# Bias sums of a fused attention and expert kernel: first block half by half, weights spread in parts, every second sum in the scores' PSUM, and the first pair started among the sums

## The chip, the cores and the metric

One Trainium2 chip, one core in use. The metric is device microseconds of one execution; of several runs the median is given. The profile is of a further execution of the same program, with its own time.

## The reference

Attention with a learned position bias, then a dense two-layer block, then eight experts weighted by a normalised gate. What matters here is the bias and the scores:

```
rel = pos[:, None] - pos[None, :]                                  # 576 x 576
x = log1p(|rel|) / log1p(max(pos, 1))[:, None]
bias = relu(x @ w1 + b1) @ w2                                      # 32 hidden units, 8 heads
scores = q @ k^T / 8 + bias;  attn = softmax(scores)               # 2 batches, 8 heads, 576 x 64
x = attn @ v  -> dense (1152 x 512, softplus, 2048 wide) -> 8 experts (1152 x 512, relu, 1024 wide)
```

## The kernel before, in words

**Bias.** A hidden unit is active or not depending on whether a query's log position lies above a threshold that depends on the distance and the unit. For every distance the kernel makes a 0/1 *mask* (128 rows: 4 distances x 32 hidden units; columns: query positions) and multiplies it on TensorE by weights that hold `w1*w2` and `b1*w2`, split into three bf16 parts. The distances are cut into five blocks (`BLOCKS`: 0, 128, 256, 384 with 128 distances and 512 with 64), each block but the last into two halves `hf` of 16 masks, and the queries into five tiles `t` of 128 rows (t = 0 is rows 0-127, t = 2 is rows 256-383, t = 4 has 64 rows). A *unit* (block, half, tile) is 16 x 3 = 48 matmuls of 64 columns into one PSUM tile of two banks (`sums`, L248); there are 40 units. After a unit ScalarE scales one half of the PSUM tile (`evac`, L259, tile `h`, L274) and VectorE adds the other half (`store`, L278, L279). When both halves of a block are in, VectorE mirrors the tile for negative distances where needed (tile `gr`, L300) and SyncE writes to a DRAM tensor `wt[t]` (L289). When all blocks of a tile are written, `read` (L1313) brings it back, skewed, as the bias of that query tile.

Every engine works through its own queue in the order in which the program is written. `seq` (L307) is the list of units. Ahead of unit n the loop at L322 emits the masks that the pace asks for (`MASK_PACE`: 32 + 3.5 n), by ScalarE ("a", L242), by VectorE in fp32 ("d", L245) or by VectorE in fp16 ("f", L240), as the letters of `MASKS` say. The "f" masks need thresholds that GpSimd computes (`thresholds`, L149). The weights of a block are split by GpSimd (`split_weights`, L199) and spread over the four distances of a mask by four VectorE instructions (`spread_weights`, L219), both at the units that `SPLIT` names. The PSUM tiles of the sums are four (tag `pac`), which is all eight banks.

**Attention.** Eight pairs (batch, two heads) go through nine steps each, one step for one query tile and head. `qk` (L426) is the score product (tile `sps`), `soft` (L448) adds the bias and takes the exponential, `norm` (L460) divides, three steps later `transp` (L484) transposes on TensorE, and `pv` (L510) multiplies by v. `prep` (L374) splits q, k and v of a pair into a rounded and a rest part: a VectorE cast (tiles `qh`, `ks`, `vx`) and GpSimd subtractions (`ql`, `ks`, `vx`). `load` (L362) brings q and k into one buffer, tag `raw`, so k of a pair is loaded when GpSimd has read q. The pair's tiles come in the order of `TILES`, beginning with tile 1. The attention's PSUM pool is opened after the pool of the sums is closed, so nothing of it starts before the last `store`.

Later parts (dense block, experts; L876, L760) are not touched.

## Time and profile before

| | |
|---|---|
| median of three runs | 1206.01 us (1205.31 to 1209.68) |
| profiled execution | 1205.54 us, its span 1203.7 us |
| TensorE matmul busy | 1172.0 us (97% of the span) |
| VectorE, ScalarE, GpSimd busy | 761.8, 560.3, 623.2 us |
| first bias matmul, last bias matmul | 11.67 us, 88.06 us from the span's start |
| first score product | 89.66 us |

In a row of a timeline the first number is the start, the second the time until the last of the merged instructions ends, both in us; xN is how many are merged; brackets give the idle time of the engine before it and what ended it. In a row of the windows the busy time of each engine in that stretch is followed by the number of instructions, then come the granted TensorE clock (1.00 is full), the share of the DMA engines that is busy and the rate.

### The profile page before, as it was taken

What the parts mean: (1) busy time and instruction counts of PE and PEld (TensorE: products, weight loads), DVE (VectorE), ACT (ScalarE), POOL (GpSimd) and SP (SyncE); (2) the same over time, 40 slices, a digit from 0 to 9 for tenths busy, and PEclk for the clock granted to TensorE, in tenths of its full rate; (3) what the DMA queues carried; (4) which work ended last, traced back from release to release, by engine and by line L of the source; (5) the groups of instructions that cost most, each with busy time, mean ns of one, the idle gap of its engine ahead of it and who ended that gap; (6) DMA issues with size and microseconds to landing.
All of it is one profiled execution on the core that took longest, in us unless ns stands there. A gap on an engine that the chain in (4) does not pass through costs nothing.

```text
span 1203.7 us, 19061 instructions
## 1 busy us (share of the span) xinstructions
PE 1172.0 (97%) x7418; PEld 993.0 (82%) x7418; DVE 761.8 (63%) x1356; ACT 560.3 (47%) x974; POOL 623.2 (52%) x533
## 2 busy tenths in 40 slices
PE   5879999999999999999999999999999999999998
PEld 5878988988888877888888888888888888888887
DVE  9967888668888765664555455555545545554554
ACT  7867877865554546325422332342233234323321
POOL 8226777657788864543453354345335534543540
PEclk9998999999999999999999999999999999999999
DMA  4676656022232211111111111111111111111102
GB/s 121 200 215 180 191 175 210 25 70 92 84 105 75 83 54 52 39 51 35 52 54 36 35 53 53 36 45 56 40 36 53 53 36 38 54 49 36 35 1 79
DMA packets 57774, 89.93 MB, mean 75 GB/s; under 512 B 7252, under 2 KB 36436, under 8 KB 57684
## 3 DMA queue, kind: packets, MB, share of 16 engines
q1 hardware_dynamic: 57252, 88.27, 23.4%
...
## 4 chain that ended last, share of the span: by engine, by line
PE 90%; DVE 4%; ACT 1%; issue 1%; POOL 1%; DMA 1%; SPq 0%; DVEq 0%; POOLq 0%; ACTq 0%
PE sum L876 36%; PE t L760 17%; PE pv L760 8%; PE tail L850 5%; PE op L529 4%; PE pv L892 4%; PE tail L760 4%; PE sps L441 3%; PE pac L255 2%; PE tp L492 2%; PE t L778 1%; DMA raw<-in_kT_dram 1%; DVE m L245 1%; PE tail L859 1%; DVE extra L279 1%
## 5 line engine op out<-in xcount | busy, mean ns | idle before, releaser
L695 POOL TENSOR_TENSOR wu<-f,wu 128x1024 fp32r<-128x1024 f32 x77 | 187.5, 2435 | 405.1 <-ACT wu L694 404.4
L876 PE MATMUL sum<-wd,h 128*128 128x512 f32 x1536 | 364.7, 393 | 0.0
L876 PEld LDWEIGHTS sum<-wd,h 128*128 128x128 f32 x1536 | 283.4, 188 | 56.3
L911 DVE SCALAR_TENSOR_TENSOR acc<-sum,prob,acc 128x512 f32<-128x512 f32 x224 | 168.1, 751 | 147.0 <-PE sum L876 147.0
L760 PE MATMUL t<-room,wu 128*128 128x512 f32 x592 | 164.6, 390 | 0.4 <-DVE u L783 0.4
L788 ACT ACTIVATE v<-t 128x512 f32<-128x512 f32 x37 | 22.1, 597 | 246.4 <-PE t L760 246.4
L760 PEld LDWEIGHTS t<-room,wu 128*128 128x128 f32 x592 | 111.1, 188 | 24.2 <-DVE u L783 0.9
L760 PE MATMUL pv<-x,wu 128*128 128x512 f32 x444 | 113.3, 391 | 0.0
L695 POOL TENSOR_TENSOR wd<-f,wd 128x1024 fp32r<-128x1024 f32 x40 | 96.4, 2410 | 8.8 <-ACT wd L694 8.1
L760 PEld LDWEIGHTS pv<-x,wu 128*128 128x128 f32 x444 | 83.0, 188 | 17.7 <-ACT u L788 0.4
L694 ACT ACTIVATE wu<-f 128x1024 fp32r<-128x1024 f32 x77 | 81.1, 1053 | 29.5 <-POOL f L691 23.6
L876 PE MATMUL sum<-h,wd 128*128 128x512 f32 x384 | 90.9, 393 | 0.0
L255 PE MATMUL pac<-bw,m 128*128 128x64 bf16 (+1 forms) x1920 | 65.8, 198 | 22.3 <-DVE bw L228 11.7
L760 PE MATMUL t<-x,wu 128*128 128x512 f32 x296 | 85.2, 389 | 0.0
L255 PEld LDWEIGHTS <-m 128*128 128x128 bf16 (+1 forms) x1920 | 62.8, 105 | 25.1 <-issue 15.0
L876 PEld LDWEIGHTS sum<-h,wd 128*128 128x128 f32 x384 | 70.6, 188 | 14.8 <-DVE acc L909 0.5
L804 ACT ACTIVATE hl<-tail 128x256 fp32r<-128x256 f32 x40 | 15.3, 383 | 142.2 <-PE tail L859 142.2
L783 DVE TENSOR_TENSOR u<-t,u 128x512 f32<-128x512 f32 x37 | 25.6, 691 | 71.8 <-PE t L760 71.8
L909 DVE TENSOR_TENSOR acc<-sum,acc 128x512 f32<-128x512 f32 x80 | 55.1, 688 | 23.9 <-PE sum L876 23.4
L760 PEld LDWEIGHTS t<-x,wu 128*128 128x128 f32 x296 | 55.6, 188 | 11.5
L783 DVE TENSOR_TENSOR tail<-tail,v 128x512 f32<-128x512 f32 x31 | 21.7, 699 | 67.4 <-PE tail L760 67.4
L458 ACT ACTIVATE p<-p,sm 128x576 f32<-128x576 f32 x72 | 55.7, 773 | 16.2 <-DVE sm L454 10.9
...
## 6 DMA issues: line engine op xcount, KB each, us to landing
f<-in_e_w_dram SPq DMA_DIRECT2D x128, 256.0 KB, 2.9
bias<-wt SPq DMA_DIRECT2D x16, 576.0 KB, 6.2
raw<-in_w_in_dram SPq DMA_DIRECT2D x16, 512.0 KB, 3.6
raw<-in_w_out_dram SPq DMA_DIRECT2D x16, 512.0 KB, 3.5
raw<-in_qT_dram SPq DMA_DIRECT2D x16, 288.0 KB, 4.8
raw<-in_kT_dram SPq DMA_DIRECT2D x16, 288.0 KB, 4.3
wt<-extra SPq DMA_DIRECT2D x9, 512.0 KB, 5.5
...
```

The costliest lines, as they stand in the source:

```text
L255: nc.tensor.matmul(pt[0:n, g], lhs, win(w, (k * (ng + 1) + gw) * NC, [[(ng - gw) * NC, 2], [1, NC]]), start=(k == 0), stop=(k == 2))
L458: nc.scalar.activation(p, p, AF.Exp, bias=sm[:, o:o + 1], scale=-1.0, accum_out=sm[:, 2 + o:3 + o])
L529: nc.tensor.matmul(op[:, 0:n], l, r, start=(part == 0 and k == 0), stop=(part == 8))
L694: nc.scalar.activation(w[:, 0], src, AF.Copy)
L695: nc.gpsimd.tensor_tensor(out=w[:, 1], in0=src, in1=w[:, 0].bitcast(F32), op=ALU.subtract)
L760: nc.tensor.matmul(zz, wu(u)[:, a, o:o + 128], xs[xn][b][j], start=(n in (1, 2, 5) and k == 0), stop=(k == 5), skip_group_check=True)
L783: nc.vector.tensor_tensor(out=out, in0=hold[bank_], in1=hold[name], op=ALU.add)
L850: nc.tensor.matmul(zr[:, 0:256], xl[:, b, k], wu(u)[:, a, 256 * k:256 * k + 256], start=(n == 0), stop=(n == 3 * KT - 1))
L876: nc.tensor.matmul(s, lhs, rhs, start=(n == 0), stop=(n == 5))
L892: nc.tensor.matmul(r, t[:, b, 128 * f:128 * f + 128], w[:, a, f], start=(n == 0), stop=(n == 5))
L909: nc.vector.tensor_tensor(out=d, in0=o, in1=d, op=ALU.add)
L911: nc.vector.scalar_tensor_tensor(out=d, in0=o, scalar=pool["prob"][:, t, e:e + 1], in1=d, op0=ALU.mult, op1=ALU.add)
```

## The change

Nothing of the arithmetic changes. The units are reordered: block 0 goes through all tiles with its first half, then with its second (`SEQ0`); block 3 (the last) ends with tile 0 instead of tile 3. Masks are emitted later (16 + 4 n, never more than the buffers that are free), in 14 buffers instead of 15. A block's weights are spread by one VectorE instruction at each of four units instead of four at one. Units with even n up to 36 take their PSUM from the two tiles of the scores (tag `s` of a pool that is opened first), the others from two tiles of their own. Attention becomes a generator: its first score product is emitted at unit 37, its step 0 at unit 38, its step 1 at unit 39. The first pair starts with tile 2. The table of the exponential is loaded after unit 33. `load` of the second pair's q is asked for earlier. Memsets of `vx` cover half the columns.

```diff
-TORDER = ((2, 4, 0, 3, 1), (0, 2, 4, 1, 3), (0, 1, 4, 2, 3), (1, 0, 4, 3, 2), (1, 3, 0, 4, 2))
-HF_MAJOR = (0, 1, 0, 0, 0)
-MASK_BUFS = 15
+TORDER = ((2, 4, 0, 3, 1), (0, 2, 4, 1, 3), (0, 1, 4, 2, 3), (3, 4, 1, 0, 2), (1, 3, 0, 4, 2))
+SEQ0 = ((0, 2), (0, 4), (0, 0), (0, 3), (0, 1), (1, 2), (1, 4), (1, 0), (1, 3), (1, 1))
+MASK_BUFS = 14
-MASK_PACE = (32, 3.5)
+MASK_PACE = (16, 4)
-SPLIT = (5, 13, 21, 26)
-PREP0 = (28, 31, 33, 34, 36)
-READS = ((4, 2), (1, 3), (3, 4), (0, 3), (2, 3))
+SPLIT = (4, 13, 21, 25)
+PREP0 = ((31, 0), (32, 2), (33, 1), (34, 3), (36, 4))
+OWN = tuple(range(1, 36, 2)) + (37, 38, 39)
+EARLY_G = 28
+AHEAD_STEPS = 2
+FIRST_STEPS = (37, 38, 39)
+TABLE_AT = 33
+READS = ((2, 3), (3, 3), (4, 3), (1, 2), (0, 2))
+TILES0 = ((2, 0), (2, 1), (3, 0), (4, 0), (3, 1), (1, 0), (0, 0), (0, 1), (1, 1))
+PVFIRST = (0, 0, 4, 7)
+PREPS1 = (1, 2, 6, 6, 7, 7)
+NORM0 = "aaapapppa"
...
-        bufs = [pool.tile([128, 3 * (128 // JJ + 1) * H * JJ], BF16, name=f"bw{n}") for n in range(4)]
+        bufs = [pool.tile([128, 3 * (128 // JJ + 1) * H * JJ], BF16, name=f"bw{n}") for n in range(3)]
...
-            for jj in range(JJ):
+            for jj in parts:
...
-        def sums(b, hf, t):
+        def sums(b, hf, t, shared):
             n = rows[t]
-            pt = pp.tile([128, HG, 2 * NC], F32, tag="pac", bufs=4, name="pac")
+            pt = ps2("pac").rearrange("p o (g c) -> p (o g) c", c=2 * NC) if shared else pp.tile(
+                [128, HG, 2 * NC], F32, tag="pac", bufs=2, name="pac")
...
-                if n == at:
-                    spread_weights(BLOCK_ORDER[k])
-                    if k < 4:
+                if at <= n < at + JJ:
+                    spread_weights(BLOCK_ORDER[k], (n - at,))
+                    if n == at + JJ - 1 and k < 4:
                         split_weights(BLOCK_ORDER[k + 1])
             need = HG * (units.index((b, hf)) + 1)
-            while made < len(todo) and made < max(need, MASK_PACE[0] + MASK_PACE[1] * n):
+            free = min([units.index(x[0:2]) for x in seq[max(n - 1, 0):]]) * HG
+            room = max(need, min(MASK_PACE[0] + MASK_PACE[1] * n, free + MG * MASK_BUFS))
+            while made < len(todo) and made < room:
...
-                    if i:
-                        load(i, "kr")
+                    load(*((i, "kr") if i else (1, "qr")))
...
-        seq = [(i, t, o) for i in range(len(pairs)) for t, o in tiles]
+        seq = [(i, t, o) for i in range(len(pairs)) for t, o in (tiles if i else TILES0)]
         lows, tails = [], []
         qk(*seq[0])
         for s in range(len(seq) + LAG + 2):
+            if s <= AHEAD_STEPS:
+                yield
...
-            for k, at_r in enumerate(PREPS):
+            for k, at_r in enumerate(PREPS if i else PREPS1):
...
+        steps = attention(env, pre, biases, read, ep, bp)
+        pa = ctx.enter_context(tc.tile_pool(name="psums", bufs=1, space=PSUM))
+        late = {n: [lambda k=k: prep(0, k)] for n, k in PREP0}
+        one = cst.tile([128, 1], F32, name="one")
+        late.setdefault(TABLE_AT, []).append(lambda: nc.scalar.activation(one, ident[:, 0:1], AF.Exp))
+        for n in FIRST_STEPS:
+            late.setdefault(n, []).append(lambda: next(steps))
```

Three places of the engines' queues follow, before and after. The first is VectorE around the four instructions that spread the weights of block 1 (`bw`; `m` masks, `h` and `pac` the sum of a unit, `g` and `extra` the bias tiles it is stored to). Before:

```order
L279 TENSOR_TENSOR g_139<-pac,h 128x2x16x16 [waits Activation_49]
L240 TENSOR_SCALAR m<-bias 128x576 [waits DVE_49,Pool_49]
L279 TENSOR_TENSOR g_139<-pac,h 128x2x16x16 [waits Activation_49]
L300 COPY gr<-g_139 128x1024 [waits DVE_49]
L240 TENSOR_SCALAR m<-bias 128x576 x2
L279 TENSOR_TENSOR g_140<-pac,h 64x32x16 [waits Activation_49]
L240 TENSOR_SCALAR m<-bias 128x576 x2
L279 TENSOR_TENSOR g_140<-pac,h 64x32x16 [waits Activation_49]
L300 COPY gr<-g_140 64x1024 [waits DVE_49]
L228 TENSOR_SCALAR bw_102<-bwp 32x396 [waits Pool_49]
```

With the change:

```order
L252 TENSOR_SCALAR m<-v,col_116 128x576 x6
L289 TENSOR_TENSOR g_141<-pac,h 128x2x16x16 [waits Activation_49]
L252 TENSOR_SCALAR m<-v,col_116 128x576 x2
L289 TENSOR_TENSOR g_142<-pac,h 64x32x16 [waits Activation_49]
L252 TENSOR_SCALAR m<-v,col_116 128x576 x2
L289 TENSOR_TENSOR extra<-pac,h 128x2x16x16 [waits Activation_49]
L235 TENSOR_SCALAR bw_106<-bwp 32x396 [waits Pool_49]
L252 TENSOR_SCALAR m<-v,col_116 128x576 x2
L289 TENSOR_TENSOR extra<-pac,h 128x2x16x16 [waits Activation_49]
L235 TENSOR_SCALAR bw_106<-bwp 32x396
```

The first spreading of block 1, which waits for GpSimd's split, moves from behind 14 fp32 masks, five fp16 masks and four stores to behind ten fp32 masks and three stores.

The second place is VectorE at the end of the sums (`sps` scores, `p` and `sm` the exponential's argument and row minimum, `qh` the cast of the next pair's q). Before:

```order
L279 TENSOR_TENSOR extra<-pac,h 64x32x16 [waits DMAHW7_49,Activation_49]
L279 TENSOR_TENSOR extra<-pac,h 64x32x16 [waits Activation_49]
L279 TENSOR_TENSOR extra<-pac,h 128x2x16x16 [waits DMAHW0_49,Activation_49]
L279 TENSOR_TENSOR extra<-pac,h 128x2x16x16 [waits Activation_49]
L454 ISA p,sm<-sps,bias 128x576 [waits DMAHW5_49,DVE_49,PE_49]
L454 ISA sm 128x1
L349 CAST qh<-raw 128x1152 [waits DMAHW4_49,DMAHW3_49,DMAHW2_49]
L454 ISA p,sm<-sps,bias 128x576 [waits DMAHW7_49,PE_49]
L454 ISA sm 128x1
```

With the change:

```order
L289 TENSOR_TENSOR extra<-pac,h 64x32x16 [waits Activation_49]
L289 TENSOR_TENSOR extra<-pac,h 128x2x16x16 [waits DMAHW1_49,Activation_49]
L289 TENSOR_TENSOR extra<-pac,h 128x2x16x16 [waits Activation_49]
L462 ISA p,sm<-sps,bias 128x576 [waits DMAHW5_49,PE_49]
L462 ISA sm 128x1
L289 TENSOR_TENSOR extra<-pac,h 128x2x16x16 [waits DMAHW4_49,Activation_49]
L462 ISA p,sm<-sps,bias 128x576 [waits PE_49]
L462 ISA sm 128x1
L471 TENSOR_SCALAR sm<-sm 128x1 [waits Activation_49]
L472 RECIPROCAL sm<-sm 128x1 [waits DVE_49]
L361 CAST qh<-raw 128x1152 [waits DMAHW6_49,DMAHW2_49,DMAHW1_49]
L289 TENSOR_TENSOR extra<-pac,h 128x2x16x16 [waits Activation_49]
```

Two bias additions of the first pair (`p,sm<-sps,bias`) and the cast of the second pair's q now stand ahead of the last store.

The third place is SyncE's queue at the same point (`wt_72` to `wt_76` are the DRAM tensors of tiles 0 to 4, `raw` is the buffer of q and k). Before:

```order
L289 DMA wt_76<-extra 512x1x128 [waits DMAHW6_49,DVE_49]
L1323 DMA bias<-wt_72 128x1152 [waits DMAHW7_49,DMAHW4_49]
L289 DMA wt_75<-extra 256x1x128 [waits DMAHW0_49,DVE_49]
L289 DMA wt_75<-extra 256x1x256
L1325 DMA bias<-wt_76 64x576 [waits DMAHW6_49,DMAHW2_49]
L1326 DMA bias<-wt_76 64x512 [waits DMAHW3_49]
L1327 DMA bias<-wt_76 64x64
L1323 DMA bias<-wt_75 128x1152 [waits DMAHW5_49,DMAHW1_49,DMAHW0_49]
L371 DMA raw<-in_kT_dram 64x1152 [waits DVE_49,Pool_49]
```

With the change:

```order
L299 DMA wt_76<-extra 512x1x128 [waits DMAHW5_49,DVE_49]
L1342 DMA bias<-wt_75 128x1152 [waits DMAHW6_49,DMAHW4_49,DMAHW3_49]
L299 DMA wt_73<-extra 256x1x128 [waits DMAHW7_49,DVE_49]
L1344 DMA bias<-wt_76 64x576 [waits DMAHW5_49,DMAHW0_49]
L1345 DMA bias<-wt_76 64x512 [waits DMAHW1_49]
L1346 DMA bias<-wt_76 64x64 [waits DMAHW2_49]
L299 DMA wt_72<-extra 512x1x256 [waits DVE_49]
L1342 DMA bias<-wt_73 128x1152 [waits DMAHW7_49]
L1342 DMA bias<-wt_72 128x1152 [waits DMAHW3_49]
L383 DMA raw<-in_kT_dram 64x1152 [waits DMAHW6_49,Pool_49]
```

The last tile written and the last one read are now tile 0's (a write of 512 rows of 256 numbers), with the read of tile 1 behind that write in the queue, and the second pair's k behind both reads.

## Rows read from the trace of the kernel before

**Rows 1.** Windows of 10 us: all engines, early, middle, and around the last sums

```profile
10.00:20.00 10.00, 7.53 (x108) 6.00 (x108) 9.93 (x19) 10.00 (x16) 8.62 (x18) 1.00 0.15 39
50.00:60.00 10.00, 8.85 (x297) 8.70 (x294) 9.84 (x28) 8.18 (x17) 0.00 (x0) 1.00 0.98 288
80.00:90.00 10.00, 5.62 (x163) 5.39 (x163) 2.96 (x5) 2.74 (x4) 1.38 (x4) 1.00 0.96 272
90.00:100.00 10.00, 8.28 (x44) 7.37 (x43) 6.83 (x20) 7.07 (x15) 7.42 (x12) 0.66 0.80 212
110.00:120.00 10.00, 10.00 (x71) 9.19 (x70) 7.79 (x23) 7.44 (x19) 5.57 (x8) 1.00 0.66 182
```

**Rows 2.** Timeline of PE, the last sums and the first scores

```profile
81.30 4.16 PE L255 MATMUL pac<-bw,m 128*64 128x64 bf16 x128 [1.43 <-issue]
86.94 1.12 PE L255 MATMUL pac<-bw,m 128*128 128x64 bf16 x33 [1.49 <-issue]
89.66 0.51 PE L441 MATMUL sps<-ks,qh 128*128 128x288 f32 x2 [1.59 <-DVE extra L279]
...
107.52 0.62 PE L441 MATMUL sps<-ks,qh 128*128 128x288 f32 x2
```

**Rows 3.** Timeline of POOL: split of block 1, subtraction of q

```profile
20.38 0.62 POOL L208 TENSOR_TENSOR bwf<-ac,lg 128x256 f32<-128x256 f32 x1
...
24.39 0.73 POOL L214 TENSOR_SCALAR bwp<-bwf 128x264 bf16<-128x264 f32 x1
...
69.39 2.83 POOL L389 TENSOR_TENSOR ql<-raw,qh 128x576 fp32r<-128x576 f32 x2 [21.25 <-DVE qh L349]
```

**Rows 4.** Timeline of DVE, first part of the sums

```profile
11.94 8.23 DVE L245 TENSOR_SCALAR m<-v,col 128x576 bf16<-128x576 f32 x14
...
21.80 0.69 DVE L300 COPY gr<-g 128x1024 f32<-128x1024 f32 x1
...
26.35 3.04 DVE L228 TENSOR_SCALAR bw<-bwp 32x396 int32<-32x396 int32 x4
...
50.77 0.65 DVE L240 TENSOR_SCALAR m<-bias 128x576 bf16<-128x576 f16 x2
```

**Rows 5.** Groups of DVE by form, 7.5 to 75.6 us

```profile
L240 DVE TENSOR_SCALAR m<-bias 128x576 bf16<-128x576 f16 x31 | 12.5, 441 | 0.1
```

**Rows 6.** Timeline of DVE, end of the sums and first pair

```profile
69.22 3.13 DVE L240 TENSOR_SCALAR m<-bias 128x448 bf16<-128x448 f16 x3
...
75.06 0.57 DVE L240 TENSOR_SCALAR m<-bias 128x448 bf16<-128x448 f16 x2
...
88.82 0.69 DVE L279 TENSOR_TENSOR extra<-pac,h 128x512 f32<-128x512 f32 x1 [2.36 <-ACT h L274]
...
97.60 0.76 DVE L454 CUSTOM_DVE_ANT_0 p<-sps,bias 128x576 f32<-128x576 f32 x1
...
100.98 0.76 DVE L349 CAST ks<-raw 128x1152 fp32r<-128x1152 f32 x1 [1.60 <-DMA raw<-in_kT_dram]
```

**Rows 7.** Timeline of ACT: unit 0, unit 33, unit 39

```profile
17.80 0.66 ACT L274 ACTIVATE h<-pac,rc 128x512 f32<-128x512 f32 x1
...
76.00 0.69 ACT L274 ACTIVATE h<-pac,rc 128x512 f32<-128x512 f32 x1 [0.71 <-PE pac L255]
...
88.11 0.69 ACT L274 ACTIVATE h<-pac,rc 128x512 f32<-128x512 f32 x1 [2.36 <-PE pac L255]
```

**Rows 8.** DMA issues, 60 to 112 us: size, median us to landing

```profile
bias<-wt SPq DMA_DIRECT2D x6, 576.0 KB, 5.7
wt<-extra SPq DMA_DIRECT2D x4, 512.0 KB, 6.0
...
raw<-in_kT_dram SPq DMA_DIRECT2D x2, 288.0 KB, 5.0
```

**Rows 9.** Timeline of SP: read of tile 3's bias

```profile
93.77 0.32 SPq L1323 DMA_DIRECT2D bias<-wt  x1
```

**Rows 10.** Window of 1 us: the granted clock in the first pair

```profile
92.00:93.00 1.00, 0.42 (x2) 0.07 (x1) 0.53 (x2) 0.99 (x2) 0.81 (x1) 0.50 0.98 192
```

More of the change, by code (lines that the diff above doesn't have):

```diff
@@ L133, in bias_setup @@
         nc.vector.tensor_scalar(ac[:, 1], w2c, b1c, 8.0, ALU.mult, ALU.mult)
+        cols = [pool.tile([128, S // JJ], F32, name=f"col{k}") for k in range(3)]
+        nc.vector.tensor_scalar(cols[0], lg, w1c, None, ALU.mult)
+        nc.vector.tensor_scalar(cols[1], cols[0], STEP_SCALE, None, ALU.mult)
+        nc.vector.tensor_scalar(v, v, b1c, None, ALU.mult)
+        nc.vector.tensor_scalar(cols[2], cols[0], -1.0, None, ALU.mult)
         sg = pool.tile([128, 4], F32, name="sg")
@@ L140, in bias_setup @@
         nc.vector.tensor_scalar(sign, sign, -1.0, None, ALU.add)
-        cols = [pool.tile([128, S // JJ], F32, name=f"col{k}") for k in range(3)]
-        nc.vector.tensor_scalar(cols[0], lg, w1c, None, ALU.mult)
-        nc.vector.tensor_scalar(cols[1], cols[0], STEP_SCALE, None, ALU.mult)
-        nc.vector.tensor_scalar(v, v, b1c, None, ALU.mult)
-        nc.vector.tensor_scalar(cols[2], cols[0], -1.0, None, ALU.mult)
         return v, lg, rc, cols, ac, bufs, sg
@@ L257, in sums, with evac @@
             return pt
-        def evac(b, hf, t, pt):
+        def evac(b, hf, t, pt, at):
             n, ng, size = rows[t], BLOCKS[b][1] // JJ, BLOCKS[b][1] * H
             if hf == 0:
+                while at >= EARLY_G and any(spare[0] is x for x in extra[0:2]):
+                    spare.pop(0)
                 gs[t] = spare[0]
@@ L335, in bias_emit @@
             held = ready
-            if n in late:
-                late[n]()
+            for fn in late.get(n, ()):
+                fn()
             if n == len(seq) - 1:
@@ L402, in prep @@
                     st.pop("kx")
-                    if i + 1 < len(pairs):
+                    if i and i + 1 < len(pairs):
                         load(i + 1, "qr")
@@ L416, in attention_pre, with attention @@
         return pairs, state, load, prep, fixed
-    def attention(sp, pre, biases, read, xr, beside, ep):
+    def attention(env, pre, biases, read, ep, bp):
         pairs, state, load, prep, fixed = pre
-        for w in range(2):
-            ts = [sp.tile([128, 4, 128], F32R, tag=f"v{x}{w}", name="vx") for x in "hl"]
-            for x in ts:
-                nc.gpsimd.memset(x.bitcast(F32), 0.0)
-            fixed.append(ts)
+        sp = xr = beside = None
+        made = []
         def qk(i, t, o):
@@ L462, in norm @@
             p, sm = st["p", t][:, S * o:S * o + S], st["sm", t]
-            (nc.vector if (EPS[r] if i < len(pairs) - 1 or r < 6 else EPSLAST[r - 6]) == "d" else nc.gpsimd).tensor_scalar(sm[:, 4 + o:5 + o], sm[:, 2 + o:3 + o], 1e-9, 0.0, ALU.add, ALU.add)
+            (nc.vector if (EPS[r] if i < len(pairs) - 1 or r < 6 else EPSLAST[r - 6]) == "d" or not i else nc.gpsimd).tensor_scalar(sm[:, 4 + o:5 + o], sm[:, 2 + o:3 + o], 1e-9, 0.0, ALU.add, ALU.add)
             nc.vector.reciprocal(sm[:, 6 + o:7 + o], sm[:, 4 + o:5 + o])
-            if NORM[r] == "a":
+            if (NORM if i else NORM0)[r] == "a":
                 nc.scalar.activation(p, p, AF.Copy, scale=sm[:, 6 + o:7 + o])
@@ L543, in attention @@
         for i in range(len(pairs)):
-            parts += [(i, ch, n) for ch in range(2) for n in range(9)]
+            parts += [(i, ch, n) for ch in (range(2) if i else (1, 0)) for n in range(9)]
         at, total = [], 0
@@ L555, in attention @@
         for s in range(len(seq) + LAG + 2):
+            if s <= AHEAD_STEPS:
+                yield
+            if s == AHEAD_STEPS:
+                sp, xr, beside = env
+                for w in range(2):
+                    ts = [sp.tile([128, 4, 128], F32R, tag=f"v{x}{w}", name="vx") for x in "hl"]
+                    for x in ts:
+                        nc.gpsimd.memset(x[:, :, 64:128].bitcast(F32), 0.0)
+                    fixed.append(ts)
             i, r = divmod(s, NT)
@@ L586, in attention @@
                 read(i // 2 + 1, AHEAD[i % 2, r])
-            beside(s, ep)
+            if s >= AHEAD_STEPS:
+                beside(s, ep)
     def experts(m0, accp, xr):
@@ L1331, in attention_moe_moe_kernel @@
         load, prep = pre[2:4]
-        late = {n: lambda k=k: prep(0, k) for k, n in enumerate(PREP0)}
+        env = []
+        steps = attention(env, pre, biases, read, ep, bp)
[5 more added lines that the diff above has]
+            late.setdefault(n, []).append(lambda: next(steps))
         with tc.tile_pool(name="bg", bufs=1) as gp, tc.tile_pool(name="btmp", bufs=1) as sp, tc.tile_pool(
@@ L1348, in attention_moe_moe_kernel @@
         with tc.tile_pool(name="att", bufs=1) as sp:
-            attention(sp, pre, biases, read, xr, beside, ep)
+            env += [sp, xr, beside]
+            for _ in steps:
+                pass
         top.close()
```

18 lines of the change are left out of this document (10 added, 8 removed).

## Prediction

> **What bounds the kernel now.** I read the windows first. From 110 us on TensorE is busy all 10.00 of 10 us, and it stays so through the span's 97%; between 10 and 20 us it is busy 7.53, between 80 and 90 us 5.62, between 90 and 100 us 8.28 at a granted clock of 0.66 [rows 1]. So whatever happens before about 107 us moves the rest as a block, and I need one mark there: the first score product of the second pair, which starts at 107.52 us, after which TensorE does not pause [rows 2]. Call it R. The prediction is what becomes of R.
>
> R has two parts. The last bias matmul ends at 86.94 + 1.12 = 88.06 us (call it T), and R comes 19.46 us behind it [rows 2].
>
> What sets T? In the windows VectorE is busy 9.93 of 10 us early and 9.84 in the middle, ScalarE 10.00 and 8.18, TensorE less [rows 1]. The masks' engines are the bound, not the matmuls, until the masks are done: the last mask (75.06 + 0.57 = 75.6 us) [rows 6] releases unit 33, whose evacuation starts at 76.00 [rows 7]. Then six units remain: 12.1 us to T, of which 1.43 and 1.49 us are pauses in which TensorE waited for nothing that shows [rows 2]. So T is the last mask + 12.5 us.
>
> What sets the 19.46 us? After the last unit come ScalarE's half (88.11, 0.69) [rows 7], VectorE's store (88.82 to 89.51) [rows 6], and only then the first score (89.66) [rows 2]; then the pair fills step by step, part of it at half clock (0.50 at 92 us) [rows 10], and the second pair's k is awaited until 100.98 [rows 6].
>
> **The change part by part.**
>
> *Backlog of VectorE at the start.* With half the masks needed for the first unit, ScalarE can evacuate it near 15 us instead of 17.80 [rows 7], and VectorE goes on with ten fp32 masks at 8.23 / 14 = 0.59 us [rows 4] and three stores at 0.6 us (0.69 us each, overlapping slightly) [rows 6]: 11.94 + 5.9 + 1.8 = 19.6 us. The next instruction in its queue is now the first spreading of block 1, and that waits for GpSimd's split, which before ran from 20.38 to 24.39 + 0.73 = 25.1 us [rows 3], behind the thresholds; nothing in the change moves that chain. VectorE's masks of the same and the next unit stand behind the wait, so it is idle for some 5 us. By 25.1 us the kernel before had done four more fp32 masks (4 x 0.59 = 2.3), five fp16 masks (5 x 0.32 = 1.6, price of the pair at 50.77) and one mirror copy (0.69) [rows 4]. So the change is 4.6 us of VectorE work behind. Bounds: 3 us if GpSimd, undisturbed, is done sooner and the first stores come later; 5.5 us if VectorE is there at 19.6 and everything is as before.
>
> *What comes back.* The 31 wide fp16 masks took 12.5 us together [rows 5]; at 0.32 us [rows 4] they would take 9.9, so 2.6 us were lost, while GpSimd ran its splits beside them. In the change most of them come after these splits. I give back 2.0 (bounds 0 and 2.6). Around 69 us three narrow masks took 3.13 us [rows 6] beside GpSimd's subtraction (69.39 to 72.22) [rows 3]; free they cost 0.57 / 2 = 0.28 each [rows 6], so 2.3 us were lost. In the change two masks, not three, follow the cast that releases the subtraction: I give back 0.9 (bounds 0 and 2.3). Together 2.9.
>
> The Trainium skill, "SBUF — State Buffer", section "Who interferes with whom", says that a VectorE instruction in its two-port modes and a GpSimd instruction exclude each other for the whole instruction, whichever starts first. By that rule the loss goes away wherever GpSimd is quiet, and the give-back would be nearly the whole 4.9 us, 2.0 us earlier than my sum; if the slow masks had another cause, nothing comes back and the sum is 2.9 us later. The trace agrees as far as it goes (3.13 us for three masks beside a subtraction, 0.57 us for two without).
>
> *Spreading in parts, order of units, three weight buffers, 14 mask buffers.* The counts are the same: as many masks of each kind, 20 spreadings, 40 units. I cost them at nothing. What hides them is the same VectorE queue, and the cover is thin: with a shorter lead of the masks, VectorE and ScalarE hand each other one unit at a time, and what one of them waits for the other adds up. Before, VectorE was idle 0.16 of 10 us in the middle [rows 1]. Bounds 0 and +4 us; I take 0, the value nearest to that row, and keep the rest for the range.
>
> So the last mask comes 4.6 - 2.9 = 1.7 us later. Then the six units follow as before, but two score products stand among them on TensorE, each two pairs of matmuls; a pair takes 0.51 us [rows 2], and as neighbours overlap by about half I take 0.53 for a product (1.0 at most): + 1.06. They wait for the casts of q and k and four half subtractions of 1.42 us [rows 3], 5.7 us in a row behind the last mask; TensorE comes to them 4 units of 1.5 us after it: just in time, so nothing more. T becomes 88.06 + 1.7 + 1.06 = 90.8 us.
>
> *The first pair.* Step 0 and most of step 1 are done at T, and the exponential's table is loaded before. What is late next is data, not TensorE. The last store ends 1.45 us after T (88.06 to 89.51) [rows 6] as before. Behind it SyncE writes tile 0 (512 KB, 6.0 us median [rows 8]; before, the last write was smaller and its read began 4.3 us after the store's end, at 93.77 [rows 9]): I take 5.5, so T + 7.0. Then the read of tile 0 is issued, and behind it k of the second pair: 5.0 us median [rows 8] with 0.5 us of issue, T + 12.5. Cast 0.76 [rows 6], GpSimd's first half 1.42 [rows 3], the semaphores' 0.1 each: T + 14.9. The bias of tile 0 lands between 3.8 us (93.77 to 97.60, which did not wait [rows 6, 9]) and 5.7 us [rows 8] after T + 7.0, so by T + 12.7, and its step is then 0.76 us of VectorE [rows 6], ahead of the cast: I take T + 15.3 for R, instead of T + 19.46. Bounds: T + 14 if the write takes 4.3; T + 18 if both the write and k take a microsecond more and the clock falls.
>
> The clock: TensorE was 0.42 busy at 92 us and at 0.50 of full speed, that is 1.2 instead of 2.4 GHz, after the windows in which it had been busy 5.62 of 10 us [rows 1, 10]. In the change it has gaps again between T and R. "TensorE: Matmul & The Clock Gate" in the Trainium skill, "Part 1: The HAM clock gate", says that the slow clock is the default and activity releases it. By that rule the sparse first pair may run at half clock once more; it would mostly fill idle time, and add 1 to 2 us to R. My upper bound holds it.
>
> At R one product with v (0.4 us) has not been done that was done before. R becomes 90.8 + 15.3 + 0.4 = 106.5 us instead of 107.5. That is 1.0 us less: 1204.5 us against the profiled execution's 1205.54, and 1205.0 against the median of 1206.0, which lies 0.5 above it.
>
> **The rivals.**
>
> *A, faster: the sums end when TensorE allows.* If VectorE's 5 us wait is taken up (later units have few masks, and all 4.9 us of blocking come back, and the unexplained pauses of 2.9 us fall away because other instructions stand there), T is about 88.06 + 1.06 + 4.6 - 4.9 - 2.9 = 85.9, and with T + 14, R is 100.3: 7.2 us less, 1198.8. For it: VectorE has 7 of 10 us free at 80 to 90 us [rows 1]. Against it: that time lies behind the last mask.
>
> *B, slower: the two mask engines go in step.* ScalarE's masks come in bursts (six at unit 11, five at unit 20, seven at unit 30), VectorE's in others; with four PSUM tiles and three `h` tiles between them a burst of one is waited for by the other. If the lead cannot absorb it, every unit takes the slower of the two. Counted unit by unit from unit 5 to 32 at 0.67, 0.35 or 0.56 us for a ScalarE mask and the VectorE prices above, the greater ones add up to 59.6 us, VectorE's alone to 49. Nothing absorbed: + 10.6; half of it: + 5.3, R = 111.8, 4.3 us more: 1210.3; three quarters: 1213. It decides from a last mask later than about 78.3 us (75.6 + 1.7 + the 1.0 gained). For it: both engines are near full [rows 1]. Against it: the kernel before has the same buffers and loses little.
>
> *C, the change doesn't do what it says:* the score products wait on TensorE's queue for the subtractions, and units 38 and 39 behind them. If GpSimd's chain comes 3 us late, T comes 3 us late, and the first pair no sooner: R = 109.5, 1208.
>
> **How the numbers follow.** The forecast, no change that counts: 0.62; A 0.20; B 0.13; C 0.05. The forecast's own range is the sum of its bounds taken together, not all at one end: - 4 to + 5 us, 1201 to 1210. To hold 8 in 10 it is widened to A's time and B's half: 1198.5 to 1211. About 0.5%, 6 us, is what a measurement of this kernel can tell from no change. Faster by more: A and a little of the forecast's low end, 0.22. Slower by more: B's upper part and some of C, 0.12. Within: 0.66.
>
> **What the profile after would show.** A wait of VectorE for GpSimd of 3 to 5.5 us before its first spreading of block 1, near 20 to 25 us. The wide fp16 masks' mean falling from 441 towards 330 ns. The last mask at 76 to 79 us, T at 89 to 92.5 us. The exponential's table load ahead of T. The second pair's k landing 12 to 14 us behind T, and R at 14 to 18 us behind T. I am wrong if the wait for GpSimd is absent or under 2 us, if T is earlier than 88 us, or if R comes less than 14 us behind T; and in the other direction if VectorE waits for ScalarE's `h` by more than 3 us in sum between 25 and 75 us.

## The result, and the profile after

The changed kernel takes 1216.08 us (median of five runs, 1215.32 to 1220.52) against 1205.63 for the kernel before in the same session: a ratio of 1.009, 95% interval 1.0067 to 1.0114. That is slower by 10.9 us by the ratio (10.5 by the medians), outside the range given. The profiled execution is the slowest of the five (1220.52 us, span 1218.6); by an estimate 3.4 us of its time come from a stall at 450 us (last section). The other four are 3.6 to 5.2 us faster; that they lack the stall is not shown, since they have no profile.

The windows of the changed kernel, which answer to [rows 1]:

```profile
20.00:30.00 10.00, 6.57 (x173) 6.20 (x170) 5.58 (x10) 8.17 (x14) 8.95 (x18) 0.88 0.01 2
30.00:40.00 10.00, 7.27 (x205) 6.65 (x202) 9.74 (x21) 8.47 (x15) 3.44 (x9) 0.95 0.69 197
40.00:50.00 10.00, 8.22 (x171) 7.82 (x172) 7.31 (x18) 5.87 (x9) 0.00 (x0) 0.66 0.97 302
110.00:120.00 10.00, 8.99 (x59) 7.67 (x59) 6.97 (x22) 5.72 (x13) 6.86 (x9) 1.00 0.54 162
```

Two things are new. Between 20 and 50 us VectorE and ScalarE, which were the bound, have idle time, and from 40 to 50 us TensorE's granted clock is 0.66 on average (0.50 from 42 to 48 us). And the last row, in which TensorE was busy 10.00 of 10, shows a pause: the second pair no longer runs dense.

TensorE's timeline, which answers to [rows 2] (start, length, what; in brackets the idle time before it and what ended it):

```profile
26.43 0.35 PE L263 MATMUL pac<-bw,m 128*128 128x64 bf16 x6 [3.19 <-DVE m L252]
...
38.23 0.91 PE L263 MATMUL pac<-bw,m 128*128 128x64 bf16 x15 [1.26 <-DVE m L247]
40.40 0.82 PE L263 MATMUL pac<-bw,m 128*128 128x64 bf16 x9 [1.26 <-DVE m L247]
42.56 7.61 PE L263 MATMUL pac<-bw,m 128*128 128x64 bf16 x162 [1.34 <-DVE m L247]
...
91.16 0.51 PE L448 MATMUL sps<-ks,qh 128*128 128x288 f32 x2
...
91.77 1.57 PE L263 MATMUL pac<-bw,m 128*128 128x64 bf16 x48
...
99.10 0.70 PE L448 MATMUL sps<-ks,qh 128*128 128x288 f32 x2 [2.84 <-DVE sm L462]
...
112.75 0.67 PE L448 MATMUL sps<-ks,qh 128*128 128x288 f32 x2
...
119.64 0.52 PE L448 MATMUL sps<-ks,qh 128*128 128x288 f32 x2 [0.51 <-DVE sm L471]
...
139.93 0.53 PE L448 MATMUL sps<-ks,qh 128*128 128x288 f32 x2 [0.97 <-DVE sm L471]
141.56 0.66 PE L500 MATMUL tp<-ident,p 128*128 128x128 f32 x4 [0.39 <-ACT p L474]
```

TensorE waits for masks four times early, 1.3 to 3.2 us each. T is 91.77 + 1.57 = 93.34 us (88.06 before), R is 112.75 (107.52). The pause at 139.93 comes back, with the same 0.97, at 178.96 and 217.46 us. One late instruction shows the sum, a group of transposes in the eighth pair, before and after:

```profile
226.35 0.66 PE L492 MATMUL tp<-ident,p 128*128 128x128 f32 x4 [0.35 <-ACT p L466]
```

```profile
237.77 0.66 PE L500 MATMUL tp<-ident,p 128*128 128x128 f32 x4 [0.39 <-ACT p L474]
```

11.4 us, of which 5.2 were there at R and 6.2 came behind it. Of the 6.2 the three pauses (0.97 + 0.39 or 0.40 us each) make 4.1. Another 1.8 are lost by the product of tile 4 in the second pair (124.63 us, 117.58 before), a stretch in which VectorE waits 1.69 us for the third pair's q (118.15 us below); before, that cast came at 110.18 us without a wait.

VectorE's timeline, which answers to [rows 4] and [rows 6]:

```profile
25.09 0.93 DVE L235 TENSOR_SCALAR bw<-bwp 32x396 int32<-32x396 int32 x1 [4.01 <-POOL bwp L223]
...
81.20 1.72 DVE L247 TENSOR_SCALAR m<-bias 128x448 bf16<-128x448 f16 x2
...
98.28 0.76 DVE L462 CUSTOM_DVE_ANT_0 p<-sps,bias 128x576 f32<-128x576 f32 x1 [2.89 <-DMA bias<-wt]
...
108.98 0.76 DVE L361 CAST ks<-raw 128x1152 fp32r<-128x1152 f32 x1
...
118.15 0.76 DVE L361 CAST qh<-raw 128x1152 fp32r<-128x1152 f32 x1 [1.69 <-DMA raw<-in_qT_dram]
...
139.11 0.76 DVE L462 CUSTOM_DVE_ANT_0 p<-sps,bias 128x576 f32<-128x576 f32 x1 [1.73 <-PE tps L506]
```

The wait for GpSimd's split is there with 4.01 us; the last mask ends at 82.9 us instead of 75.6. The last row is the cause of the pause on TensorE: a bias addition waits for transposes (L506) that read the score buffer it wants to write.

### The profile page after: what moved, and what is told of

Its sections match the earlier page's. It is cut to its first block, busy times and chain, and to the rows that moved or that the text cites. A ratio compares the mean times of both kernels' runs of the same rounds, so it can differ in the third digit from the quotient of the medians.

```text
span 1218.6 us, 19062 instructions
## 1 busy us (share of the span) xinstructions
PE 1176.5 (97%) x7418; PEld 995.6 (82%) x7418; DVE 762.2 (63%) x1358; ACT 562.0 (46%) x978; POOL 618.0 (51%) x527
## 4 chain that ended last, share of the span: by engine, by line
PE 89%; DVE 4%; POOL 2%; ACT 2%; DMA 1%; issue 1%; SPq 0%; POOLq 0%; DVEq 0%; ACTq 0%
PE sum L895 36%; PE t L779 16%; PE pv L779 8%; PE tail L869 4%; PE pv L911 4%; PE op L537 4%; PE tail L779 4%; PE pac L263 3%; PE sps L448 2%; PE tp L500 2%; PE t L797 1%; PE tail L878 1%; DVE p L462 1%; DVE m L247 1%; ACT m L249 1%
## 5 line engine op out<-in xcount | busy, mean ns | idle before, releaser
L263 PE MATMUL pac<-bw,m 128*128 128x64 bf16 (+1 forms) x1920 | 68.9, 200 | 23.6 <-DVE bw L235 12.2
L263 PEld LDWEIGHTS <-m 128*128 128x128 bf16 (+1 forms) x1920 | 65.3, 106 | 26.9 <-ACT m L249 10.1
L823 ACT ACTIVATE hl<-tail 128x256 fp32r<-128x256 f32 x40 | 15.3, 384 | 141.8 <-PE tail L878 141.8
```

Source lines behind the costliest of these rows:

```text
L263: nc.tensor.matmul(pt[0:n, g], lhs, win(w, (k * (ng + 1) + gw) * NC, [[(ng - gw) * NC, 2], [1, NC]]), start=(k == 0), stop=(k == 2))
```

## The experiments

Medians moved by a microsecond between sessions, so the table gives the excess over the kernel before as (ratio - 1) x 1205.6 us; its 95% intervals are +-1.1 to +-2.8 us, widest for the changed kernel. T, R and the starts of the ten-matmul tile-4 product of the 2nd, 3rd and 4th pair are from the one profiled execution of each kernel. T moves by a microsecond even where the sums are the same (88.06 before and 89.20 in e17, 93.34 after and 94.00 in e13).

| kernel | ratio (95%) | excess us | T | R | tile 4 of pairs 2, 3, 4 |
|---|---|---|---|---|---|
| before | | 0 | 88.06 | 107.52 | 117.58, 135.82, 154.70 |
| after | 1.0090 (1.0067-1.0114) | 10.9 | 93.34 | 112.75 | 124.63, 145.47, 163.81 |
| a_bias_part | 1.0051 (1.0034-1.0068) | 6.1 | 95.84 | 115.52 | 125.58, 143.97, 162.41 |
| b_attention_part | 1.0064 (1.0047-1.0080) | 7.7 | 86.69 | 105.68 | 120.59, 140.49, 158.91 |
| e1_spread_later | 1.0102 (1.0084-1.0121) | 12.3 | 91.36 | 111.82 | 124.50, 145.35, 163.54 |
| e2_load_behind | 1.0079 (1.0061-1.0097) | 9.5 | 91.82 | 110.67 | 122.27, 143.18, 161.40 |
| e5_prep_early | 1.0044 (1.0032-1.0056) | 5.3 | 88.51 | 110.22 | 119.95, 140.44, 158.64 |
| e6_raw_twice | 1.0043 (1.0030-1.0056) | 5.2 | 91.56 | 114.00 | 123.74, 143.59, 161.82 |
| e8_early_loads | 1.0046 (1.0033-1.0059) | 5.5 | 87.19 | 109.29 | 119.06, 139.51, 157.71 |
| e7_lead | 1.0016 (1.0005-1.0028) | 1.9 | 90.21 | 110.39 | 120.44, 138.67, 157.69 |
| e9_p_pools | 1.0018 (1.0009-1.0028) | 2.2 | 86.64 | 105.82 | 118.27, 138.13, 156.99 |
| e10_pools_prep | 1.0016 (1.0006-1.0025) | 1.9 | 88.53 | 111.09 | 120.83, 139.39, 158.28 |
| e11_three | 1.0029 (1.0019-1.0039) | 3.5 | 87.21 | 109.32 | 119.05, 137.95, 156.88 |
| e12_k_on_pool | 1.0026 (1.0014-1.0038) | 3.1 | 88.28 | 112.26 | 122.00, 141.36, 160.20 |
| e13_whole_pools | 1.0066 (1.0054-1.0078) | 8.0 | 94.00 | 115.67 | 126.40, 145.52, 164.45 |
| e14_whole_pools_lead | 1.0034 (1.0023-1.0045) | 4.1 | 88.83 | 108.49 | 121.04, 140.17, 159.06 |
| e15_k_between | 1.0029 (1.0018-1.0041) | 3.5 | 86.71 | 107.97 | 119.69, 138.67, 157.58 |
| e16_all | 1.0039 (1.0026-1.0052) | 4.7 | 87.00 | 108.98 | 121.64, 140.67, 159.55 |
| e17_old_two_pools | 1.0028 (1.0017-1.0038) | 3.4 | 89.20 | 108.33 | 118.38, 138.41, 156.65 |
| e18_old_short_lead | 1.0018 (1.0003-1.0032) | 2.2 | 89.58 | 108.72 | 118.76, 137.00, 155.92 |

**The two halves.** a_bias_part is the kernel before with the sums' half of the change alone (`SEQ0`, `MASK_PACE`, `MASK_BUFS`, `SPLIT`, spreading in parts, three weight buffers); b_attention_part is the changed kernel with that half undone, except that it keeps the 14 mask buffers and the three weight buffers.

> The kernel before with the bias half of the change alone: block 0 half by half, block 1 tile by tile, weights spread in parts from units 4, 13, 21, 25, the shorter mask lead, three weight and 14 mask buffers. PSUM, last tile and attention are as before. Theory 1 (the sums lose the time: VectorE stands 4 us at the first spreading of block 1, TensorE then starves and its clock halves): the last bias matmul comes 4 to 6 us later than in the kernel before, and so does the end: about 1210 to 1212. Theory 2 (the attention half loses it): the sums end within 1 us of before, 1204 to 1207.

> The changed kernel with the bias half undone: order of blocks 0 and 1, mask lead (32 + 3.5 n) and spreading in one go as before; shared PSUM, tile 0 last, first pair from tile 2 and first steps among the sums stay. Theory 1: no wait for GpSimd near 21 us, the last bias matmul 4 to 6 us earlier than in the changed kernel, near 88 to 89 us; the whole near 1210, or as before if the first pair is no loss. Theory 2 (the first pair loses it, since the write of tile 3 stands behind the second pair's q in SyncE's queue): as slow as the changed kernel, 1214 to 1217.

Both halves lose. The first loses ahead of T: its T is 7.8 us late and everything behind it runs at the old distance (R - T is 19.7). The second reaches T and R earlier than before, by 1.4 and 1.8 us, and loses behind R: it is 3.0 us late by the 2nd pair's tile 4 and 4.7 by the 3rd's. So R, on which the prediction stood, says nothing of the second half's loss. The two losses, 6.1 and 7.7 us, do not simply add up to the whole's 10.9.

**The wait for GpSimd: e1_spread_later** (whole change).

```diff
-SPLIT = (4, 13, 21, 25)
+SPLIT = (6, 13, 21, 25)
```

> The changed kernel with one number changed: the spreading of block 1 starts at unit 6 instead of unit 4. Theory 1: VectorE no longer stands 4.0 us before it, TensorE does not starve between 35 and 42 us, its clock stays at 1.00 there, and the last bias matmul comes 4 to 6 us sooner: 1210 to 1212. Theory 2: the freed time is given back at the masks' end, at most 1 us is won.

VectorE's wait falls from 4.01 to 0.97 us. T comes 2.0 us earlier than in the changed kernel, but R only 0.9 and the 2nd pair's tile 4 only 0.1, and the time is no better. The edit trades one wait for another, so it is no test of the first alone: TensorE now waits 5.61 us for the last part of the same spreading, and from 30 to 40 us its granted clock is 0.64 on average:

```profile
34.48 4.17 PE L263 MATMUL pac<-bw,m 128*128 128x64 bf16 x72 [5.61 <-DVE bw L235]
```

**The mask lead: e7_lead** (a_bias_part with the old lead) and **e18_old_short_lead** (the kernel before with the new one).

```diff
-MASK_PACE = (16, 4)
+MASK_PACE = (32, 3.5)
```

> The sums half alone (a_bias_part), with the old mask lead: MASK_PACE = (32, 3.5) for (16, 4), still capped by the free mask buffers. Theory 'short lead': TensorE's 7 us of waits for masks between 25 and 45 us come from the lead of 16 masks; expected waits below 2 us there, the granted clock at 0.8 or more between 30 and 50 us, T at 88 to 91 us (95.84 in the half alone, 88.06 before) and a time of 1206 to 1209 us. Rival 'half by half': with the first block's rows run half by half, block 1's weights and masks are wanted before GpSimd has split them; then VectorE still waits 3 to 5 us for the split at the first spreading, T stays at 93 to 96 us and the time at 1211 to 1214.

> The old kernel with the mask lead of the change alone: MASK_PACE = (16, 4) for (32, 3.5), the first block still run as before and with 15 mask buffers. Theory 'short lead': masks are made just in time from unit 1 on, TensorE waits for VectorE's masks between 20 and 45 us as in the whole change, and the last bias product ends 3 to 6 us later than 88.06: 1208 to 1211 us. Rival 'lead matters only with the half-by-half order': within 1 us of 1205.4.

With the old lead the sums' half loses 1.9 us instead of 6.1, though its units still go half by half, and its wait for GpSimd falls to 1.0 us by itself. The window from 40 to 50 us, of a_bias_part and then of e7_lead:

```profile
40.00:50.00 10.00, 7.90 (x200) 7.45 (x198) 8.03 (x18) 6.33 (x11) 0.00 (x0) 0.77 0.95 285
```

```profile
40.00:50.00 10.00, 8.65 (x269) 8.40 (x269) 9.81 (x23) 7.16 (x11) 0.16 (x1) 1.00 1.08 321
```

VectorE, the bound, is busy 9.81 again, and TensorE keeps its full clock. Put alone into the kernel before, the short lead costs 2.2 us (0.4 to 3.9; T + 1.5, little more than T moves by itself), and there the one waited for is ScalarE's mask (3.5 us), not VectorE's as I had expected. The short lead costs by itself. It costs more with the new order of units (4.2 us for 2.2), though the intervals overlap.

**The score buffers: e9_p_pools, e13_whole_pools, e17_old_two_pools.** Lines of the change that the excerpt ahead of the prediction leaves out, and to which the prediction gave no term:

```diff
-                st["p", t] = sp.tile([128, 2 * S], F32, tag="p", bufs=4, name="p")
+                st["p", t] = (sp if len(made) & 2 else bp).tile([128, 2 * S], F32, tag="p", bufs=2, name="p")
+                made.append(t)
```

The four buffers stay four, but two belong to the bias pool and two to the attention's, dealt by turns of two tiles. e9 (on b_attention_part) and e13 (on the whole change) deal them by another pattern; e17 is the kernel before with its four buffers in two such groups and nothing else.

```diff
+                st["p", t] = (bp if ("bbssb", "bssbs")[len(made) // 5 % 2][len(made) % 5] == "b" else sp).tile(...)
```

> The attention half alone (b_attention_part) with the four score buffers p, which the change deals two to the bias pool and two to the attention pool by turns of two, dealt so that the second tile of a pair gets the buffer of a tile that was done early in the pair before (tiles 1, 0, 3, 4, 2 of a pair to pools b, b, s, s, b and in the next pair b, s, s, b, s). Theory 'buffers': in the 3rd, 5th and 7th pair (near 134, 173 and 212 us) VectorE waits 1.7 us for the transposes of the tile (3,1) of the pair before, and TensorE pauses 0.97 + 0.40 us each time, because both buffers that this pool may give are late; the old kernel, with all four in one pool, has no such pause. Expected: these three pauses gone (TensorE busy 9.9 of 10 us or more in 130 to 140 and 170 to 180), 4.1 us less, 1209 to 1211 us. Rival 'the pair is too full': the pauses come from the late loads and casts and only move; then the time stays within 1.5 us of 1214.2.

> The whole changed kernel with one repair: the score buffers dealt as in e9_p_pools. Theory 'buffers': the same pauses at 139.9, 179.0 and 217.5 us go, 5.9 us as in the attention half (1214.2 to 1208.3); 1209 to 1212 us expected for 1216.1. Rival 'hidden in the whole': since the whole is later at the second pair already, less than 2 us come back and it stays at 1214 or above.

> The old kernel with one thing of the change alone: its four score buffers dealt in two groups of two, by turns of two tiles, as the change deals them between its two pools. Nothing else differs. Theory 'buffers': the second tile of the 3rd, 5th and 7th pair finds only the late buffer, VectorE waits for the transposes of tile (3,1) and TensorE pauses 1.37 us each time, near 128, 166 and 205 us; 3 x 1.37 = 4.1 us or, by what undoing it brought in the attention half, 5.9: 1209.5 to 1211.5 us expected for 1205.4. Rival 'only with the new first pair': the old kernel has slack there and stays within 1 us of 1205.4.

e17 settles it: the old kernel gets the same pauses, at 132.86, 171.76 and 210.58 us, each 0.97 + 0.39 or 0.40, from the same wait of VectorE, and is 3.4 us slower; 3 x 1.37 = 4.1 lies in its interval (2.0 to 4.6). VectorE, then TensorE in e17:

```profile
132.04 0.76 DVE L456 CUSTOM_DVE_ANT_0 p<-sps,bias 128x576 f32<-128x576 f32 x1 [1.72 <-PE tps L500]
```

```profile
132.86 0.53 PE L442 MATMUL sps<-ks,qh 128*128 128x288 f32 x2 [0.97 <-DVE sm L456]
```

A pair has five tiles, in the order 1, 0, 3, 4, 2. In the 3rd, 5th and 7th pair tiles 1 and 0 both draw from the pool whose buffers the pair before left with its tiles 0 and 3, and tile 3, finished last of all, is still being transposed. With four in one pool tile 0 gets the buffer of tile 4, long done: in the program of the kernel before, the score buffer of the third pair's tile 0 has the address of the second pair's tile 4, and in the programs of the changed kernel and of e17 that of its tile 3. In e9 two of the three pauses are gone and the first is down to 0.40 (TensorE busy 9.46, 9.99 and 10.00 of 10 us from 130, 170 and 210 us). It brought back 5.5 us in the half; e13 brought back 2.9 in the whole, where the intervals overlap.

**The loads of the next pairs: e2, e5, e6, e15.** e2_load_behind is the whole change with the q loads asked for where the kernel before asks; e5, e6 and e15 stand on b_attention_part (e15 with e9's buffers).

```diff
 e5:  -PREPS1 = (1, 2, 6, 6, 7, 7)   +PREPS1 = (0, 0, 4, 4, 4, 7)
 e6:  -tag "raw", 1 buffer, MASK_BUFS = 14   +tag "raw", 2 buffers, MASK_BUFS = 13
 e15: -PREPS1 = (1, 2, 6, 6, 7, 7)   +PREPS1 = (1, 1, 6, 6, 7, 7)
```

> The changed kernel with the loads of q as before: the second pair's q is asked for after the fourth part of the first pair's preparation (behind the write of tile 3 in SyncE's queue), and the third pair's as before. Theory 2: the write of tile 3 goes out near 84 us instead of 88.88, its read lands before VectorE asks for it, the wait of 2.89 us in the first pair is gone, and the mark R (the first score product of the second pair) comes 2 to 4 us sooner: 1212 to 1214. Theory 1: R is set by the reads of tile 0 and of the second pair's k, which stay where they are: at most 1 us is won.

> The attention half alone (b_attention_part), with the second pair's preparation at the steps that the later pairs have: PREPS1 = (0, 0, 4, 4, 4, 7) for (1, 2, 6, 6, 7, 7). Theory 'late preparation': the attention half reached R 1.8 us before the old kernel (105.68 for 107.52), and lost its time behind R because the loads and casts of the 2nd and 3rd pair come late. Expected: the k load of the 2nd pair and the q load of the 3rd are issued 3 to 5 us earlier (91 to 94 and 102 to 104 us for 96.41 and 106.74), the ten-matmul tile-4 products of pairs 1, 2, 3 start at about 117, 135 and 154 us (120.6, 140.5, 158.9 in the half alone; 117.6, 135.8, 154.7 before), and the time is 1204 to 1208 us. Rival 'other order': the new row order, the norms on ScalarE and the later value products of the first pair cost it; then those three starts stay within 1 us of 120.6, 140.5, 158.9 and the time at 1213 to 1216.

> The attention half alone, with two buffers for the raw q and k in place of one (one mask buffer fewer, 13, and the mask lead capped by what is free, to make room). Theory 'one buffer': the chain load, cast, subtract, load through a single buffer is as long as a pair (about 19 us for 18.25) and can't catch up; with two, the idle of TensorE behind R goes: the starts of pair 2 and 3 follow that of pair 1 by 18.2 to 18.6 us each (19.9 and 18.4 in the half alone), and the time falls by 4 us or more, to 1206 to 1210, less what the smaller mask lead costs at T (read at T: 86.69 in the half alone). Rival 'order of SP's queue and of the steps': the loads wait for their place behind the bias reads and not for the buffer; then the load of the 2nd pair's k is still issued at 96 to 97 us and the time stays at 1213 to 1216.

> e9_p_pools with the second pair's first two parts at step 1 (PREPS1 = (1, 1, 6, 6, 7, 7)): the k load of the 2nd pair then stands in SP's queue behind tile 4's bias reads and ahead of tile 0's write and the reads of tiles 1 and 0. Theory 'SP's queue': k is issued at 92 to 94 us (96.52 in e9_p_pools), the tile-4 products of pairs 1 and 2 start 1 to 2 us earlier than 118.27 and 138.13, and the time is 1205 to 1207 (1208.3 in e9_p_pools). Rival 'the bias rows': tile 0's write and the reads behind it are held up by as much as k gains; no change or 1 us slower.

None gained what its theory said. In e2 VectorE's wait for tile 3's bias falls from 2.89 to 0.16 us, as expected, and R comes 2.1 us earlier; but T does too, by 1.5, so that R - T is only 0.6 us shorter, and the time is better by nothing that its interval shows. In e5 k was issued at 91.38 us as expected and the loss fell by 2.4 us (the intervals overlap), but R came 4.5 us later than in the half (T 1.8 later): k now stands ahead of tile 4's bias reads, and the first pair waits for them. e15, with k at 91.31 us, is no faster than e9 with k at 96.5: the reads of tiles 1 and 0 behind it keep up the first pair instead. e6's k was issued at 98.95 us, later than in the half, with T 4.9 us later; it is inconclusive, since the smaller mask buffer moved the sums as well. Another, e8, gave e5 the old places of the q loads: 1211.16 us, like e5. And e10, e9 with e5's steps, took 1207.14 us, by the ratio no faster than e9.

So each load put forward put a bias row back. That the order in SyncE's queue alone does this is not shown, and e12 speaks against it. It is e10 with k issued from GpSimd's queue (at 91.75 us; 91.85 in e10), so that tile 4's bias reads left SyncE's queue 1.3 us earlier (91.79 us for 93.05). VectorE nevertheless got that bias 1.2 us later. Its addition for tile 4, in e10 and then in e12:

```profile
98.72 0.76 DVE L465 CUSTOM_DVE_ANT_0 p<-sps,bias 128x576 f32<-128x576 f32 x1 [3.23 <-DMA bias<-wt]
```

```profile
99.89 0.76 DVE L465 CUSTOM_DVE_ANT_0 p<-sps,bias 128x576 f32<-128x576 f32 x1 [4.25 <-DMA bias<-wt]
```

The last of these reads took 6.8 us to land instead of 4.2, and the time, 1208.28 us, is no better. The rival that was named ahead of e12 is that the transfers themselves are the limit (the share of the DMA engines is 1.05 from 95 to 100 us in both). It fits, and was not tested further.

**Both repairs in the whole: e14_whole_pools_lead, e11_three.** e14 has e9's buffers and the lead (32, 3.5); e11 has e5's steps as well.

> The whole changed kernel with two repairs: the score buffers dealt as in e9_p_pools and the mask lead of the old kernel (32, 3.5). Additive: 1216.1 less 5.9 less 5.9 is 1204.3; 1203 to 1207 expected. If the earlier preparation of e11_three was what kept that kernel at 1209.2 (it puts the 2nd pair's k load ahead of tile 4's bias reads), this one is 2 us or more below it; if something else is left in the whole, it is at 1208 to 1211 as well.

> The whole changed kernel with three repairs: score buffers dealt as in e9_p_pools, the second pair's preparation as in e5_prep_early, the mask lead of the old kernel as in e7_lead. If the loss is the sum of these three causes: 1216.1 less 4.1 less 2.6 less 5.9 is 1203.5; 1202 to 1209 expected, since the halves do not add up exactly (their losses alone are 7 and 8.4 us, the whole loses 10.5). If something is left that only the whole has, 1211 or above.

The two repairs bring back 6.8 of 10.9 us: 2.9 by the buffers (e13), 3.9 more by the lead. 4.1 us (2.8 to 5.4) stay, and my sum, 1204.3, was wrong by that. In e14 T and R are within 1 us of the kernel before, and the 2nd pair's tile 4 is 3.5 us late. SyncE's issues of q and k, then the casts on VectorE that wait for them, in e14:

```profile
98.96 1.14 SPq L383 DMA_DIRECT2D raw<-in_kT_dram  x2
...
109.85 1.11 SPq L383 DMA_DIRECT2D raw<-in_qT_dram  x2
```

```profile
106.09 0.76 DVE L361 CAST ks<-raw 128x1152 fp32r<-128x1152 f32 x1 [1.45 <-DMA raw<-in_kT_dram]
...
114.57 0.76 DVE L361 CAST qh<-raw 128x1152 fp32r<-128x1152 f32 x1 [1.57 <-DMA raw<-in_qT_dram]
```

Before, k was issued at 95.00 and q at 104.73 us: 6.9 behind T and 2.8 ahead of R, now 10.1 behind T and 1.4 behind R. That these late loads are the rest is not shown: in e11, with the earlier steps, k was issued at 89.95 us (T + 2.7) and q at 103.73 (5.6 ahead of R), and the time is the same, 1209.2 us. What the remaining 4.1 us are stays open. e16, which adds e15's order to e14, took 1210.33 us, and no version beats the kernel before; the nearest are e7, e9 and e10 (e9 with e5's steps), at 1.0016 to 1.0018.

## Why the prediction was wrong

*"After which TensorE does not pause."* This step failed, and with it the plan to forecast one mark. It was true of the kernel before [rows 1, 2] and was carried over without asking what holds it up: free score buffers and the third pair's q in time. The change touches both. 6.2 us of the 11.4 at 226 us were lost behind R, where the forecast had none. e17 shows the part of the buffers; the part of the third pair's q is read from VectorE's wait of 1.69 us, and no run tests it alone. The other 5.2 us are R's, which was forecast 1.0 us earlier and came 5.2 later (below). For the buffers the order of the instructions showed it beforehand: the bias addition for tile 0 of the third pair waits in the kernel before on TensorE alone and in the changed one on ScalarE as well,

```
before  L454 ISA p_3116,sm_3117<-sps_3071,bias_2761 128x576 [waits PE_49]
after   L462 ISA p_3119,sm_3120<-sps_3074,bias_2751 128x576 [waits PE_49,Activation_49]
```

because its buffer's last user is the tile that ScalarE has just normalised and TensorE is about to transpose.

*The wait for GpSimd* was right: 3 to 5.5 us forecast, 4.01 measured, at the place named. But its length is not the price: in e1 it falls to 0.97 us and the time stays, because other waits take its place, and with the old lead (e7) it shrinks to 1.0 us by itself.

*The give-back of 2.9 us* came in part. Of the 2.0 us for the wide fp16 masks 0.2 came; their mean is 442 ns (441 before [rows 5]), forecast 330:

```profile
L247 DVE TENSOR_SCALAR m<-bias 128x576 bf16<-128x576 f16 x31 | 12.3, 442 | 0.1
```

They left one split of GpSimd and met the next. The same group from 40 to 52 us, with GpSimd busy 0.00, and from 52 to 62, with GpSimd busy 3.66 us:

```profile
L247 DVE TENSOR_SCALAR m<-bias 128x576 bf16<-128x576 f16 x11 | 3.5, 360 | 0.0
```

```profile
L247 DVE TENSOR_SCALAR m<-bias 128x576 bf16<-128x576 f16 x12 | 5.6, 513 | 0.0
```

The Trainium skill, "SBUF — State Buffer", section "Who interferes with whom", lets only one of the two engines at the shared port; the trace agrees with 360 against 513 ns. The rule was right, and I had placed the wide masks wrongly. The narrow ones gave back more than I took, 1.4 us for 0.9. Before, then after:

```profile
L240 DVE TENSOR_SCALAR m<-bias 128x448 bf16<-128x448 f16 x16 | 6.9, 468 | 0.0
```

```profile
L247 DVE TENSOR_SCALAR m<-bias 128x448 bf16<-128x448 f16 x16 | 5.5, 398 | 0.0
```

*"I cost them at nothing"*, of order, lead and buffers in the sums: the bounds were 0 and + 4 us. The last mask came at 82.9 us, 7.3 later than before and 5.6 later than my sum. With 4.0 us for the wait and 1.6 given back, 4.9 are left for this term, beyond its upper bound. VectorE's waits for ScalarE's `h` up to the last mask are 4.9 us (0.9 before). Rival B had named the place (the two mask engines without a cushion), its deciding point (a last mask later than 78.3) and R = 111.8; R was 112.75. That the two come so near is luck: by B's sum T would have been 96.1 (90.8 + 5.3), and it was 93.34; the rest came between T and R. Its sign, that wait between 25 and 75 us, was 3.1 us against 0.9 before, just over the 3 that I had named. What it missed is the clock. TensorE was busy 0.68, 0.89 and 0.78 us in the three stretches of 2 us from 36 to 42 us; from 42 to 48 us its granted clock was 0.50, that is 1.2 GHz. It was then itself waited for: up to the last mask ScalarE waited 11.9 us for sums in the changed kernel, 2.8 before. How much of the 4.9 us is the clock's, no run separates. One stretch at the low clock, then ScalarE's waits in the changed kernel (us in total, times, longest):

```profile
42.00:44.00 2.00, 1.44 (x28) 1.45 (x29) 1.38 (x4) 0.00 (x0) 0.00 (x0) 0.50 1.05 349
```

```profile
ACT h L284 <- PE pac L263: 11.9, 12, 2.7
```

*T* was forecast as the last mask plus 12.5 + 1.06; measured 82.9 + 10.4 = 93.34: the two unexplained pauses of [rows 2] (1.43 and 1.49 us) are gone, as rival A had allowed, so that T is 2.5 us later than forecast and not 5.6. The two score products cost 0.61 us each from their start to that of the next sum (89.14 to 89.75 and 91.16 to 91.77 us), 1.2 us for 1.06. The exponential's table is loaded at 83.98 us, ahead of T, as forecast.

*R = T + 15.3* was T + 19.4. The largest mis-sized term is SyncE's queue, 2.4 of the 4.1 us: I let tile 0's write start 1.45 us behind T and k 7.0.

```profile
87.23 1.60 SPq L383 DMA_DIRECT2D raw<-in_qT_dram  x2
...
90.23 0.60 SPq L299 DMA_DIRECT2D wt<-extra  x1
93.54 0.34 SPq L1342 DMA_DIRECT2D bias<-wt  x1
...
95.92 0.48 SPq L1344 DMA_DIRECT2D bias<-wt  x1
...
97.72 0.60 SPq L299 DMA_DIRECT2D wt<-extra  x1
98.42 4.19 SPq L1342 DMA_DIRECT2D bias<-wt  x2
102.70 1.14 SPq L383 DMA_DIRECT2D raw<-in_kT_dram  x2
...
113.31 1.11 SPq L383 DMA_DIRECT2D raw<-in_qT_dram  x2
```

The second pair's q load holds the queue until 88.83, then tile 3's read waits for tile 3's write until 93.54 and tile 4's reads for tile 4's write (90.23) until 95.92; tile 0's write went at 97.72, T + 4.4, and k at 102.70, T + 9.4. I had priced what each instruction waits for and not what stands in front of it in its queue. The rest came behind: k's cast began 6.3 us after its issue (5.5 forecast), and GpSimd began its half 0.7 us after that cast (0.1 forecast), once it had done a norm. e2 took the q load out of the way, and R - T fell by 0.6 us only, so the waits for the writes weigh more than that load. The last row is the third pair's q, 0.56 us behind R.

*Rival A* (1198.8) is out: T is later, not earlier, though its pauses did go. *Rival C* is out: the score products at 89.14 and 91.16 us waited for nothing. The chance of 0.12 for slower by more than 0.5% was too small, since the sum ended at R and had no term for what the change does behind it, the dealing of the score buffers above all.
